# Hand-overs between row halves: new places, SyncE or VectorE, and 17 more of them, in a hand-ordered attention and MoE kernel

## The chip, the cores and the metric

The kernel runs on one core of one Trainium2 chip. The metric is the device time of one execution in microseconds (us); less is better. A core has five engines that run side by side, each with its own in-order queue, and that signal each other by semaphores: TensorE (PE: matmuls, and PEld, the loading of their weights), VectorE (DVE), ScalarE (ACT), GpSimd (POOL) and SyncE (SP). SyncE computes nothing here; it issues DMAs and waits.

## The reference

Softcapped attention over 8 batches, 12 heads, 448 tokens and a head size of 64, and on its result a layer that takes the larger of two products and multiplies it by a third matrix:

```python
scores = scale * (q @ k.T)                 # per batch and head, 448 x 448
scores = cap * tanh(scores / cap)          # cap = 30
attn   = softmax(scores)
x      = attn @ v                          # rearranged to 3584 tokens x 768
out    = maximum(x @ w1, x @ w2) @ w_out   # w1, w2: 768 x 1024, w_out: 1024 x 768
```

Inputs and output are float32; the kernel works in bfloat16 with float32 sums.

## The kernel before

*What is computed.* The maximum is written as x @ w2 + relu(x @ (w1 - w2)), and x @ w2 @ w_out is one product with a matrix wm = w2 @ w_out that is made at the start. The attention goes by pairs of heads i (48 of them), and two pairs make a t (24). For each pair: scores `S` (line 514), tanh `T` (519) and exp `E` (536) on ScalarE, with `L`, `TL`, `EL` for the 64 left-over rows; sums of the exponentials by adds on VectorE (`A` at 548, `B` at 553) and a product with ones (`Y`, "the totals", 573); the product with v (`VL` at 600, `V` at 606); the inverse of the totals (`Y1` to `Y3`, 578 to 584); and the scaling `N` (618, 621) into xT. Scores lie in two PSUM tiles, so that new scores wait until ScalarE has read old ones.

*The second part* has 120 groups of matmuls, numbered through: for each of 8 batches 8 groups of stage 1 (x times a slice of w1 - w2, 6 steps of 448 columns, ended by a relu on VectorE at line 666, `ev`) and 6 or 8 of stage 2 (a slice of the output: 6 steps with wm and 8 with w_out, 384 columns, ended by a copy at 700 or 702, and stored by SyncE at 676 to 681, `st`). Each group sums in one PSUM bank; there are four banks for groups, totals and the like (`O g bank` opens group g).

*Row halves.* A matmul with 64 rows uses half of TensorE's rows, and two such matmuls, one on each half, run at the same time. So each step of a group is cut into its upper and its lower 64 rows, and `M x y n` runs n steps of the upper half of group x and of the lower half of group y, in turn (line 645; 640 is a whole step). A group therefore does one half of all its steps first and the other half later, or goes to and fro: it is transferred from one row half to the other 145 times in all.

*The hand-over.* [...] A hand-over of group g is an empty instruction on another engine (line 654): `Hs g` puts it on SyncE, `H g` on VectorE. It waits for the last matmul of the old half, and the first weight load of the new half waits for it. Since TensorE's queue is in order, a late hand-over stops all that stands behind that weight load. Where no hand-over is written, nothing waits, and only the matmuls in between keep the two apart.

```python
        def step(self, h):
            ...
            ins = nc.tensor.matmul(self.ps, w[r], x[r], start=first, stop=self.at == [self.n, self.n]).ins
            if self.last is not None and self.last[0] != h:
                if self.turn is not None:
                    tc.add_manual_dep(ins, self.turn.name, BANK, reason="bank")
                self.turn = None
            self.last = (h, ins)

        def hand_over(self, eng):

            self.turn = eng.nop().ins
            tc.add_manual_dep(self.turn, self.last[1].name, BANK, reason="bank")
```

*What sets the order.* There is no scheduler: `ORDER`, a string at the top of the file, lists all steps, and each engine's queue takes its instructions in this order. So the place of an `Hs` sets what stands before and behind it on SyncE: other hand-overs, the stores, and from t = 5 on the DMA transposes (`cr`, line 475), which turn q and k from kqs into qkT. A transpose waits for its loads and for its buffer; the loads of a later t (`lk`, `lq`, 328, issued by GpSimd) wait until the transpose has read theirs. The place of an `H` sets what stands around it on VectorE.

Of the kernel before, what the change touches and what calls it, by code (L numbers as in the profile page):

```python
# [21 lines left out]
S 5 0; X 6 0; E 4 0 3; T 5 0; EL 2; Y1 1; Y2 1; PC 2 1; Y3 1; N 1 1; N 1 0; XC 6; X 7 2; W 4 1; S 5 2; S 5 1;
X 8 0; P 3 1 3; WC 4; XC 8; PC 3 1; T 5 1; T 5 2; OP 4 0 1; P 4 0 2; OP 0 1 0; P 0 1 3; S 6 0; S 6 1; W 5 3;
P 0 1 1; P 4 0 6; P 0 1 4; E 5 0 2; T 6 1; T 6 0; E 5 2 3; XC 7; sub 2 0; WC 5; sub 4 0; PC 4 0; sub 0 0; PC 0 1;
OP 5 1 3; P 5 1 4; S 6 2; L 3; Y 2 1; T 6 2; TL 3; E 6 0 3; VL 2; V 2 1 0 1; V 2 0 0 3; V 2 1 1 3; S 7 0; P 5 1 4;
OP 5 0 0; P 5 0 8; Y1 2; Y2 2; Y3 2; N 2 0; N 2 1; A 3 0 1; A 3 0 2; PC 5 1; PC 5 0; T 7 0; EL 3; lk 9 0; lq 11 0;
lv 3 1; lq 9 0; lw1 1; lw1 3; lq 10 0; lk 12 1; lv 3 0; lw1 5; lk 10 0; lk 11 0; lk 11 1; lk 10 1; S 7 2; O 0 1;
M 0 -1 2; S 7 1; M 0 -1 4; O 1 2; M 1 -1 1; T 7 2; T 7 1; Hs 0; M 1 -1 1; S 8 1; M 1 -1 1; M 1 0 3; S 8 0; X 9 3;
OP 4 1 0; P 4 1 4; sub 1 0; sub 3 0; XC 9; T 8 1; E 7 0 2; T 8 0; E 7 2 3; P 4 1 4; L 4; O 2 3; M 2 0 3; S 8 2;
M 2 1 3; A 3 1 1; B 3 1; PC 4 1; ev 0; B 3 0; Hs 2; TL 4; T 8 2; O 3 0; M 3 1 3; M 3 2 1; S 9 0; M 3 2 2; T 9 0;  # L30
E 8 0 3; ev 1; A 3 1 2; sub 5 0; cr 5; Hs 3; O 4 1; M 4 2 1; VL 3; V 3 0 0 3; Y 3 2; V 3 1 0 3; M 4 2 2; S 9 1;
M 4 3 3; lk 13 0; lk 13 1; lv 4 1; lv 4 0; lv 5 3; lv 5 0; lq 13 0; lq 15 0; lq 12 0; lk 12 0; lk 15 1; Y1 3;
Y2 3; Y3 3; ev 2; Hs 4; O 5 2; M 5 3 3; M 5 4 3; T 9 1; EL 4; ev 3; N 3 0; N 3 1; Hs 5; O 6 3; M 6 4 3; M 6 5 2;
# [745 lines left out]
```

## Time and profile before

| what | value |
|---|---|
| time, three executions | 328.19, 328.49, 328.52 us; median 328.49 |
| span of the profiled execution (first to last instruction) | 326.9 us |
| median beyond that span | 1.59 us |
| busy: TensorE, ScalarE, VectorE, GpSimd | 320.2, 281.1, 240.1, 162.2 us |
| matmuls | 4138 |
| hand-overs on SyncE, on VectorE | 107, 21 |

In the profile a row of a timeline has the start and the duration in us, the engine, the line, the operation with what it writes and reads, and a count. A row of the views of waits says who waited for whom: total us, times, the longest. "SPq" and "DVEq" are the engines' queues: instructions that wait or issue and do no work. A busy TensorE is not TensorE at its peak, since matmuls overlap.

### The profile page before, as it was taken

What the parts mean: (1) busy time and instruction counts of PE and PEld (TensorE: products, weight loads), DVE (VectorE), ACT (ScalarE), POOL (GpSimd) and SP (SyncE); (2) the same over time, 40 slices, a digit from 0 to 9 for tenths busy, and PEclk for the clock granted to TensorE, in tenths of its full rate; (3) what the DMA queues carried; (4) which work ended last, traced back from release to release, by engine and by line L of the source; (5) the groups of instructions that cost most, each with busy time, mean ns of one, the idle gap of its engine ahead of it and who ended that gap; (6) DMA issues with size and microseconds to landing.
All of it is one profiled execution on the core that took longest, in us unless ns stands there. A gap on an engine that the chain in (4) does not pass through costs nothing.

```text
span 326.9 us, 9772 instructions
## 1 busy us (share of the span) xinstructions
PE 320.2 (98%) x4138; PEld 184.5 (56%) x4138; DVE 240.1 (73%) x422; ACT 281.1 (86%) x278; POOL 162.2 (50%) x237
## 2 busy tenths in 40 slices
PE   7999999999999999999999999999999999999994
PEld 3454545545656664565565565556466556557662
DVE  3346899987997778987897788968878779773201
ACT  5999999999999999999999999999999999921120
POOL 7357584568772772764774474478448311000000
PEclk9999999999999999999999999999999999999999
DMA  8999999899999999999999999999999963013033
GB/s 179 174 202 185 269 256 112 92 140 116 221 188 98 134 182 191 102 99 175 163 176 108 208 114 181 128 140 182 183 116 101 201 156 45 2 50 98 0 98 96
DMA packets 134508, 46.28 MB, mean 142 GB/s; under 512 B 112321, under 2 KB 129473, under 8 KB 134465
## 3 DMA queue, kind: packets, MB, share of 16 engines
q0 software_dynamic: 94592, 25.02, 78.3%
q1 hardware_dynamic: 39424, 19.99, 31.1%
q8 instruction: 32, 0.52, 0.6%
q10 hardware_dynamic: 448, 0.66, 0.5%
q14 instruction: 12, 0.09, 0.1%
HBM read 47.78 MB, written 11.01 MB: 180 GB/s over the span
## 4 chain that ended last, share of the span: by engine, by line
PE 93%; DMA 3%; POOL 1%; DVE 1%; issue 0%
PE mm L645 61%; PE s L514 9%; PE s L606 9%; PE mm L431 5%; DMA w2b<-in_moe_w_dram 3%; PE s L528 2%; PE s L600 2%; PE mm L573 2%; PE mm L640 1%; POOL kqs L321 1%; PE mm L458 1%; PE mm L566 1%; PE mm L416 0%; DVE xT L621 0%; POOL w2b L366 0%; DVE xT L618 0%
## 5 line engine op out<-in xcount | busy, mean ns | idle before, releaser
L519 ACT ACTIVATE e<-s 128x896 bf16<-128x896 f32 x144 | 125.5, 927 | 5.7 <-PE s L514 5.2
L536 ACT ACTIVATE e<-e 128x1792 bf16<-128x1792 bf16 (+2 forms) x72 | 122.7, 1709 | 0.0
L645 PE MATMUL mm<-wo_sb,gT 64*128 64x384 bf16 x864 | 115.2, 323 | 0.0
L645 PE MATMUL mm<-wm_sb,xT 64*128 64x384 bf16 x648 | 102.2, 323 | 0.0
L645 PE MATMUL mm<-xT,wd_sb 64*128 64x448 bf16 x768 | 97.5, 349 | 0.0
L328 POOL DMA_DIRECT2D kqs<-in_k_dram x76 | 54.7, 722 | 56.1 <-DMA qkT<-kqs 50.9
L645 PEld LDWEIGHTS <-gT 64*128 64x128 bf16 x864 | 58.6, 94 | 25.5 <-issue 1.1
L645 PEld LDWEIGHTS <-wd_sb 64*128 64x128 bf16 x768 | 48.8, 94 | 26.7 <-issue 2.1
L645 PEld LDWEIGHTS <-xT 64*128 64x128 bf16 x648 | 50.3, 94 | 18.5 <-issue 0.2
L514 PE MATMUL s<-qkT 64*128 64x448 bf16 x288 | 52.7, 352 | 0.2 <-DVE xT L618 0.2
L352 POOL DMA_DIRECT2D vp<-in_v_dram x48 | 30.5, 639 | 32.6 <-PE s L514 23.5
L666 DVE TENSOR_SCALAR gT<-mm 128x448 bf16<-128x448 f32 x64 | 38.9, 617 | 8.7 <-PE mm L645 7.6
L328 POOL DMA_DIRECT2D kqs<-in_q_dram x38 | 35.1, 924 | 5.7 <-issue 2.5
L606 PE MATMUL s<-e,vp 128*32 128x448 bf16 x576 | 36.1, 354 | 0.0
L548 DVE TENSOR_TENSOR esum<-e 128x896 bf16<-128x896 bf16 x42 | 25.9, 617 | 9.1 <-ACT e L536 9.1
L621 DVE TENSOR_TENSOR xT<-s,inv 64x448 bf16<-64x448 f32 x48 | 29.9, 622 | 1.7 <-PE s L606 0.8
L548 DVE TENSOR_TENSOR esum<-esum,e 128x896 bf16<-128x896 bf16 x42 | 26.2, 623 | 5.9 <-ACT e L536 4.8
L514 PEld LDWEIGHTS <-qkT 64*128 64x128 bf16 x288 | 18.5, 94 | 20.1 <-issue 12.0
L700 ACT COPY osb<-mm 128x384 f32<-128x384 f32 x10 | 4.8, 479 | 26.9 <-PE mm L645 26.7
L702 DVE COPY osb<-mm 128x384 f32<-128x384 f32 x44 | 23.3, 554 | 6.2 <-PE mm L645 5.7
L553 DVE TENSOR_TENSOR esum<-esum,el 64x896 bf16<-64x896 bf16 x42 | 26.0, 619 | 1.2
L578 DVE STREAM_TRANSPOSE st<-mm 128x448 f32<-128x448 f32 x24 | 15.6, 649 | 13.0 <-PE mm L573 11.3
(57 smaller groups left out, 269.7 us busy)
## 6 DMA issues: line engine op xcount, KB each, us to landing
out_dram<-osb SPq DMA_DIRECT2D x54, 192.0 KB, 4.5
vp<-in_v_dram POOLq DMA_DIRECT2D x38, 160.0 KB, 4.3
kqs<-in_q_dram POOLq DMA_DIRECT2D x46, 112.0 KB, 5.8
kqs<-in_k_dram POOLq DMA_DIRECT2D x76, 56.0 KB, 4.4
osb<-in_moe_w_dram POOLq DMA_DIRECT2D x4, 512.0 KB, 7.4
w2b<-in_moe_w_dram POOLq DMA_DIRECT2D x6, 256.0 KB, 7.1
wo_sb<-in_moe_w_out_dram POOLq DMA_DIRECT2D x4, 384.0 KB, 9.9
vp<-in_v_dram POOLq DMA_DIRECT2D x10, 128.0 KB, 7.7
```

Source lines behind the costliest of these rows:

```text
L328: nc.gpsimd.dma_start(out=to, in_=x)
L352: nc.gpsimd.dma_start(out=to, in_=x)
L514: scored[i, j] = nc.tensor.matmul(s[:, h, :S], k_of(t, o, h, j), q_of(t, o, h)).ins
L519: nc.scalar.activation(expo[i][:, 2 * j : 2 * j + 2, :], slots[i, j][:, :, :S], AF.Tanh, scale=scale / cap)
L536: nc.scalar.activation(e, e, AF.Exp, scale=float(cap))
L548: nc.vector.tensor_add(d, e[:, 0:2, :] if j == 1 else d, e[:, 2 * j : 2 * j + 2, :])
L553: nc.vector.tensor_add(d, d, left_e[t][r, :, :])
L606: nc.tensor.matmul(vals[t][place(m, u), u, :S], w[:, m, :], expo[2 * t + o][:, 2 * j + h, :], start=False, stop=(j == NJ - 1))
L621: nc.vector.tensor_mul(x[64 - r : 128 - r], vals[t][r : r + 64, u, :S], sums[t, 3][64 - r : 128 - r])
L645: ins = nc.tensor.matmul(self.ps, w[r], x[r], start=first, stop=self.at == [self.n, self.n]).ins
L666: nc.vector.tensor_relu(gT[b // 2][:, f, cs], ps)
L702: nc.vector.tensor_copy(o[:, hs], ps)
```

## The change

All steps of `ORDER` but the hand-overs are the same, in the same order; a count in `M` is split where a hand-over now falls inside it. So every matmul, activation, copy and DMA keeps its place among those of its engine.

All 145 transfers now have a hand-over, where 128 had. 96 are on SyncE (107 before), 49 on VectorE (21). Of the 128, 73 stay on SyncE and 9 on VectorE, 34 go from SyncE to VectorE and 12 from VectorE to SyncE; 19 keep both engine and place. The 17 added ones are those of groups 1, 10, 12, 17, 24, 42, 70, 72, 77, 84 and 87 on SyncE and of 27, 40, 47, 54, 57 and 102 on VectorE, each from the upper to the lower half. In ten of them 25 matmuls of groups lie from the last of the old half to the first of the new one, in seven 9.

The core of the diff, at three places, rows cut to the steps that matter:

```diff
-O 36 1; M 36 34 1; lk 27 0; M 36 34 1; A 10 0 1; Hs 35; M 36 34 1; E 21 0 2; M 36 35 1; S 22 1; ev 34; lk 27 1;
-M 36 35 2; O 37 3; M 37 35 1; A 10 0 2; M 37 35 1; Hs 36; lq 27 0; M 37 35 1; M 37 36 2; T 22 0; ev 35; M 37 36 1;
-O 38 2; M 38 36 1; A 10 1 1; M 38 36 1; Hs 37; cr 12;
+O 36 1; M 36 34 1; H 35; lk 27 0; M 36 34 1; A 10 0 1; M 36 34 1; E 21 0 2; M 36 35 1; S 22 1; ev 34; lk 27 1;
+M 36 35 2; H 36; O 37 3; M 37 35 1; A 10 0 2; M 37 35 1;
...
-M 46 44 1; st 2 1; M 46 44 1; Hs 45; T 26 1; cr 14; B 12 0;
-T 26 2; O 47 0; M 47 45 2; H 46; M 47 45 1;
+M 45 43 2; ev 42; lk 31 1; M 45 43 1; M 45 44 2; ev 43; M 45 44 1; H 45; T 26 0;
...
-Hs 66; lq 39 0; M 67 65 1; M 67 66 2; T 34 0; ev 65; M 67 66 1; O 68 0; M 68 66 1; A 16 1 1; M 68 66 1; Hs 67;
+M 66 65 2; O 67 3; M 67 65 1; H 66; A 16 0 2; M 67 65 1; lq 39 0; M 67 65 1; M 67 66 2; T 34 0; ev 65;
+M 67 66 1; O 68 0; M 68 66 1; H 67; A 16 1 1; M 68 66 1; cr 18;
```

In the second place the hand-over of group 46 follows the transpose `cr 14` on SyncE (`Hs 46`). The one edit outside `ORDER` is in `transposes`, and leaves every call as it was:

```diff
-        if c != 1:
+        if bank is not None:
             turned["qk", i] = mm_tile(bank).bitcast(bf16)
```

More of the change, by code (lines that the diff above doesn't have):

```diff
@@ new lines @@
+E 1 2 3; E 1 0 2; TL 1; T 2 0; EL 0; S 3 0; S 2 2; P 3 0 1; W 0 2; P 3 0 1; X 4 3; T 2 2; T 3 0; VL 0; Y 0 1;
+V 0 0 0 3; V 0 1 0 3; S 3 1; lwo 1 0; lwo 1 1; lq 5 0; lk 5 0; lv 1 0; lv 1 1; lk 8 0; lq 8 0; lq 7 0; lw2 4;
+lv 6 2; lq 6 0; lk 7 0; lk 6 0; lw2 5; lw1 2; lw1 4; lw1 0; lv 2 0; lv 2 1; WC 0; PC 3 0; XC 4; Y1 0; Y2 0;
+Y3 0; N 0 0; N 0 1; E 2 0 3; T 3 1; EL 1; E 3 0 2; OP 0 0 1; P 0 0 2; OP 2 1 2; P 2 1 2; P 0 0 1; OP 1 1 3;
+P 1 1 2; P 0 0 1; P 1 1 2; P 0 0 1; P 1 1 4; S 4 0; S 3 2; X 5 0; P 2 1 4; P 0 0 3; P 2 1 1; XC 5; PC 1 1;
@@ new lines @@
+TL 4; T 8 2; O 3 0; M 3 1 3; M 3 2 1; S 9 0; M 3 2 2; T 9 0; E 8 0 3; ev 1; A 3 1 2; sub 5 0; cr 5; O 4 1;
+M 4 2 1; VL 3; V 3 0 0 3; Y 3 2; Hs 3; V 3 1 0 3; M 4 2 2; S 9 1; M 4 3 3; lk 13 0; lk 13 1; lv 4 1; lv 4 0;
+lv 5 3; lv 5 0; lq 13 0; lq 15 0; lq 12 0; lk 12 0; lk 15 1; Y1 3; Y2 3; Y3 3; ev 2; O 5 2; M 5 3 2; Hs 4;
+M 5 3 1; M 5 4 3; T 9 1; EL 4; ev 3; Hs 5; N 3 0; N 3 1; O 6 3; M 6 4 3; M 6 5 2; S 10 0; M 6 5 1; O 7 0;
+M 7 5 3; Hs 6; ev 4; A 4 0 1; ev 5; M 7 6 2; S 9 2; M 7 6 1; Hs 7; cr 6; E 9 0 2; T 10 0; T 9 2; O 8 1; M 8 6 3;
@@ new lines @@
+M 16 15 1; T 14 2; O 17 2; M 17 15 1; H 16; M 17 15 2; B 6 1; M 17 16 2; E 13 2 3; M 17 16 1; ev 15; O 18 3;
+M 18 16 1; L 7; VL 6; A 6 1 2; st 0 2; TL 7; V 6 0 0 2; V 6 1 0 2; Hs 17; Y 6 0; E 14 0 3; V 6 0 2 3; V 6 1 2 3;
+Y1 6; S 15 0; M 18 16 1; lv 8 0; M 18 16 1; Y2 6; M 18 17 1; Y3 6; M 18 17 1; lv 8 1; M 18 17 1; O 19 0;
+M 19 17 1; Hs 18; M 19 17 1; ev 16; lv 8 2; M 19 17 1; M 19 18 1; T 15 0; N 6 0; M 19 18 2; lv 8 3; O 20 1;
+M 20 18 2; EL 7; ev 17; M 20 18 1; lk 20 0; Hs 19; S 15 1; M 20 19 1; N 6 1; M 20 19 1; T 15 1; M 20 19 1;
@@ new lines @@
+L 8; VL 7; A 7 1 2; TL 8; V 7 0 0 2; V 7 1 0 2; Y 7 2; E 16 0 3; V 7 0 2 3; lk 22 0; V 7 1 2 3; Y1 7; S 17 0;
+M 22 23 1; Hs 24; lv 9 0; M 22 23 1; Y2 7; M 22 23 2; Y3 7; M 22 23 1; lv 9 1; M 22 23 2; O 25 2; M 25 23 1;
+N 7 0; M 25 23 1; lv 9 2; M 25 23 1; T 17 0; M 25 24 1; N 7 1; M 25 24 2; lv 9 3; M 25 24 2; EL 8; M 25 24 1;
+S 17 1; lk 22 1; M 25 24 2; ev 22; M 25 24 1; T 17 1; S 17 2; lq 22 0; M 25 24 1; ev 23; M 25 24 1; O 26 3;
+M 26 24 1; T 17 2; M 26 24 1; H 25; A 8 0 1; S 18 0; M 26 24 1; lk 23 0; M 26 25 1; A 8 0 2; M 26 25 1;
@@ new lines @@
+S 21 2; S 22 0; M 35 34 1; ev 33; T 21 2; M 35 34 1; O 36 1; M 36 34 1; H 35; lk 27 0; M 36 34 1; A 10 0 1;
+M 36 34 1; E 21 0 2; M 36 35 1; S 22 1; ev 34; lk 27 1; M 36 35 2; H 36; O 37 3; M 37 35 1; A 10 0 2; M 37 35 1;
+lq 27 0; M 37 35 1; M 37 36 2; T 22 0; ev 35; M 37 36 1; O 38 2; M 38 36 1; A 10 1 1; M 38 36 1; cr 12;
+M 38 36 1; T 22 1; Hs 37; M 38 37 1; S 22 2; B 10 0; M 38 37 2; Hs 38; T 22 2; O 39 0; M 39 37 1; ev 36;
+M 39 37 2; B 10 1; E 21 2 3; M 39 38 3; ev 37; L 11; VL 10; TL 11; V 10 0 0 2; A 10 1 2; V 10 1 0 2; Y 10 1;
@@ new lines @@
+E 22 0 3; V 10 0 2 3; V 10 1 2 3; Y1 10; lk 28 0; S 23 0; M 39 38 2; Y2 10; M 39 38 1; lv 12 0; M 39 38 1;
+Y3 10; M 39 38 3; lv 12 1; M 39 38 1; N 10 0; O 40 3; M 40 38 2; T 23 0; Hs 39; M 40 38 1; Hs 38; lv 12 2;
+N 10 1; M 40 39 3; M 38 39 1; EL 11; lv 12 3; H 40; M 38 39 1; S 23 1; M 38 39 2; lk 28 1; A 11 0 1; M 38 39 1;
+T 23 1; S 23 2; M 38 39 2; A 11 0 2; lq 28 0; M 38 39 1; T 23 2; O 41 1; M 41 39 1; S 24 0; ev 38; M 41 39 2;
+M 41 40 1; lk 29 0; E 23 0 2; M 41 40 1; ev 39; S 24 1; M 41 40 2; lk 29 1; M 41 40 5; lq 29 0; M 41 40 1;
@@ new lines @@
+M 52 50 1; Hs 51; lk 33 0; M 52 50 1; A 13 0 1; M 52 50 1; M 52 51 1; E 27 0 2; M 52 51 1; lk 33 1; ev 50;
+S 28 1; M 52 51 1; H 52; O 53 1; M 53 51 1; A 13 0 2; M 53 51 1; lq 33 0; M 53 51 1; M 53 52 2; ev 51;
+M 53 52 1; T 28 0; M 53 52 2; A 13 1 1; M 53 52 2; cr 15; M 53 52 1; T 28 1; M 53 52 1; B 13 0; S 28 2;
+M 53 52 2; H 53; B 13 1; O 54 2; M 54 52 1; T 28 2; M 54 52 2; M 54 53 1; Hs 52; E 27 2 3; M 54 53 2; M 52 53 1;
+H 54; L 14; VL 13; A 13 1 2; TL 14; V 13 0 0 2; V 13 1 0 2; Y 13 0; E 28 0 3; V 13 0 2 3; lk 34 0; V 13 1 2 3;
@@ new lines @@
+Y1 13; S 29 0; M 52 53 1; lv 15 0; M 52 53 1; Y2 13; M 52 53 2; Y3 13; M 52 53 1; lv 15 1; M 52 53 2; O 55 0;
+M 55 53 1; N 13 0; M 55 53 1; lv 15 2; M 55 53 1; T 29 0; M 55 54 1; N 13 1; M 55 54 2; lv 15 3; M 55 54 2;
+EL 14; M 55 54 1; S 29 1; lk 34 1; M 55 54 2; ev 52; M 55 54 1; T 29 1; S 29 2; lq 34 0; M 55 54 1; ev 53;
+M 55 54 1; H 55; O 56 3; M 56 54 1; T 29 2; M 56 54 1; A 14 0 1; S 30 0; M 56 54 1; Hs 54; lk 35 0; M 56 55 1;
+A 14 0 2; M 56 55 1; E 29 0 2; M 56 55 1; S 30 1; lk 35 1; M 54 55 5; lq 35 0; M 54 55 3; T 30 0; O 57 1;
@@ new lines @@
+EL 15; lv 16 3; M 59 58 1; S 31 1; M 59 58 2; lk 36 1; ev 56; M 59 58 1; T 31 1; S 31 2; M 59 58 1; ev 57;
+M 59 58 1; lq 36 0; M 59 58 1; T 31 2; M 59 58 1; A 15 0 1; S 32 0; M 59 58 2; A 15 0 2; M 59 58 1; lk 37 0;
+E 31 0 2; O 60 3; M 60 58 1; S 32 1; M 60 58 2; H 59; H 58; lk 37 1; M 60 59 3; Hs 60; M 58 59 1; lq 37 0;
+M 58 59 1; T 32 0; M 58 59 1; A 15 1 1; M 58 59 1; cr 17; M 58 59 2; B 15 0; M 58 59 1; T 32 1; M 58 59 1;
+S 32 2; O 61 1; M 61 59 1; ev 58; M 61 59 1; T 32 2; M 61 59 1; B 15 1; M 61 60 3; Hs 61; st 3 5; E 31 2 3;
@@ new lines @@
+ev 59; O 62 2; M 62 60 3; L 16; ev 60; VL 15; TL 16; V 15 0 0 2; A 15 1 2; V 15 1 0 2; E 32 0 3; M 62 61 1;
+Y 15 0; V 15 0 2 3; V 15 1 2 3; lk 38 0; Y1 15; S 33 0; M 62 61 2; Y2 15; lv 17 0; O 63 3; M 63 61 1; st 3 6;
+Hs 62; Y3 15; M 63 61 2; lv 17 1; M 63 62 1; T 33 0; N 15 0; M 63 62 2; lv 17 2; O 64 0; M 64 62 1; ev 61;
+M 64 62 1; EL 16; M 64 62 1; Hs 63; S 33 1; lv 17 3; N 15 1; M 64 63 3; T 33 1; lk 38 1; O 65 1; M 65 63 2;
+Hs 64; M 65 63 1; M 65 64 1; ev 62; lq 38 0; S 33 2; S 34 0; M 65 64 1; ev 63; T 33 2; M 65 64 1; O 66 2;
@@ new lines @@
+cr 19; M 72 70 2; Hs 70; B 17 0; T 36 1; M 72 71 1; S 36 2; M 72 71 2; B 17 1; M 70 71 1; T 36 2; M 70 71 5;
+st 4 0; E 35 2 3; M 70 71 2; O 73 1; M 73 71 1; ev 70; L 18; VL 17; A 17 1 2; TL 18; Hs 72; V 17 0 0 2;
+V 17 1 0 2; Y 17 3; E 36 0 3; V 17 0 2 3; V 17 1 2 3; Y1 17; S 37 0; lk 42 0; M 73 71 2; Y2 17; M 73 72 2;
+Y3 17; lv 19 0; M 73 72 4; N 17 0; lv 19 1; M 73 72 2; T 37 0; M 73 72 1; N 17 1; M 73 72 1; lv 19 2; M 73 72 1;
+Hs 73; O 74 3; M 74 72 2; EL 18; S 37 1; lv 19 3; M 74 72 1; Hs 72; M 74 73 1; ev 71; M 74 73 1; T 37 1;
@@ new lines @@
+M 82 83 1; Y2 19; M 82 83 2; Y3 19; Hs 84; M 82 83 1; lv 21 1; M 82 83 2; O 85 1; M 85 83 1; N 19 0; M 85 83 1;
+lv 21 2; M 85 83 1; T 41 0; M 85 84 1; N 19 1; M 85 84 2; lv 21 3; M 85 84 2; EL 20; M 85 84 1; S 41 1; lk 46 1;
+M 85 84 2; ev 82; M 85 84 1; T 41 1; S 41 2; lq 46 0; M 85 84 1; ev 83; M 85 84 1; O 86 3; M 86 84 1; T 41 2;
+M 86 84 1; H 85; A 20 0 1; S 42 0; M 86 84 1; lk 47 0; Hs 84; M 86 85 1; A 20 0 2; M 86 85 1; E 41 0 2;
+M 86 85 1; S 42 1; lk 47 1; M 84 85 4; Hs 86; M 84 85 1; lq 47 0; M 84 85 3; T 42 0; O 87 2; M 87 85 1;
@@ new lines @@
+S 43 1; M 89 88 2; ev 86; M 89 88 1; T 43 1; S 43 2; M 89 88 1; ev 87; M 89 88 2; T 43 2; M 89 88 1; A 21 0 1;
+S 44 0; M 89 88 2; A 21 0 2; M 89 88 1; E 43 0 2; O 90 3; M 90 88 1; S 44 1; M 90 88 2; Hs 89; H 88; M 90 89 3;
+M 88 89 2; T 44 0; M 88 89 1; A 21 1 1; M 88 89 1; cr 23; M 88 89 2; B 21 0; M 88 89 1; T 44 1; M 88 89 1;
+S 44 2; H 90; O 91 2; M 91 89 1; ev 88; M 91 89 1; T 44 2; M 91 89 1; B 21 1; M 91 90 3; st 5 5; E 43 2 3;
+ev 89; O 92 0; M 92 90 3; L 22; Hs 91; ev 90; VL 21; TL 22; V 21 0 0 2; A 21 1 2; V 21 1 0 2; E 44 0 3;
@@ new lines @@
+M 92 91 1; Y 21 1; V 21 0 2 3; V 21 1 2 3; Y1 21; S 45 0; M 92 91 1; lv 23 0; M 92 91 1; Y2 21; O 93 3;
+M 93 91 1; st 5 6; Y3 21; Hs 92; M 93 91 1; lv 23 1; M 93 91 1; M 93 92 1; T 45 0; N 21 0; M 93 92 1; lv 23 2;
+M 93 92 1; O 94 1; M 94 92 1; ev 91; M 94 92 1; EL 22; lv 23 3; Hs 93; M 94 92 1; S 45 1; N 21 1; M 94 93 3;
+T 45 1; O 95 2; M 95 93 1; Hs 94; M 95 93 2; M 95 94 1; ev 92; S 45 2; S 46 0; M 95 94 1; ev 93; T 45 2;
+M 95 94 1; O 96 0; M 96 94 2; A 22 0 1; M 96 94 1; Hs 95; E 45 0 2; M 96 95 1; S 46 1; ev 94; M 96 95 2; O 97 3;
@@ new lines @@
+Hs 100; M 98 99 2; EL 23; M 98 99 1; S 47 1; M 98 99 2; A 23 0 1; M 98 99 1; T 47 1; S 47 2; M 98 99 2;
+A 23 0 2; O 101 0; M 101 99 1; T 47 2; M 101 99 2; ev 98; M 101 100 3; ev 99; E 47 0 2; M 101 100 8; O 102 1;
+M 102 100 1; Hs 101; M 102 100 1; E 47 2 3; M 102 100 1; A 23 1 1; H 100; M 102 101 3; B 23 0; VL 23;
+V 23 0 0 2; B 23 1; V 23 1 0 2; A 23 1 2; M 100 101 1; st 6 0; M 100 101 4; Y 23 2; V 23 0 2 3; V 23 1 2 3;
+Y1 23; M 100 101 3; H 102; Y2 23; O 103 2; M 103 101 2; Y3 23; eva 100; M 103 101 1; M 103 102 2; eva 101;
@@ L202 @@
+M 117 115 1; M 117 116 2; eva 115; M 117 116 5; st 7 4; M 117 116 4; M -1 116 2; H 117; M -1 116 1; M -1 117 2;
+H 116; M -1 117 1; M 116 117 8; M -1 117 2; eva 116; M -1 117 1; O 118 1; M 118 118 1; eva 117; M 118 118 6;
+st 7 5; M 118 118 7; O 119 2; M 119 119 2; ev 118; M 119 119 12; ev 119; st 7 6;
 """
```

298 lines of the change are left out of this document (112 added, 186 removed).

## The prediction

> **What bounds the kernel now.** I read the page first, then the busy time by window, then the views of waits, and last the timelines around single hand-overs.
>
> ```profile
> span 326.9 us, 9772 instructions
> PE 320.2 (98%) x4138; PEld 184.5 (56%) x4138; DVE 240.1 (73%) x422; ACT 281.1 (86%) x278; POOL 162.2 (50%) x237
> ACT  5999999999999999999999999999999999921120
> ```
>
> TensorE (PE) fills the span. ScalarE (ACT) is full for 34 of the 40 slices, to about 285 us. Then it is nearly idle and TensorE works off what is left alone.
>
> ```profile
> 189.70:260.00 70.30, 70.30 (x924) 41.22 (x920) 58.09 (x103) 68.39 (x67) 42.66 (x60) 1.00 1.35 153
> ```
>
> This stretch of the middle is 70.30 us long; the fourth busy time, 68.39, is ScalarE's. It idles 1.9 us in 70, so two chains bind each other: TensorE needs score banks that ScalarE has emptied, and ScalarE needs scores. A delay of TensorE counts where ScalarE is waiting for it.
>
> ```profile
> ACT e L519 <- PE s L514: 5.2, 9, 0.8
> SPq L654 <- PE mm L645: 218.7, 103, 48.0
> SPq L475 <- PE mm L645: 19.4, 14, 2.3
> ```
>
> ScalarE waits 9 times for TensorE's scores, 5.2 us in all (total, count, longest). SyncE (SPq) spends 218.7 us in hand-overs (L654), as it should: it stands ready before the matmul ends. The last row is their side effect: 14 of 19 DMA transposes (L475) stood behind hand-overs, 1.4 us each on average.
>
> ```profile
> L654 SPq EVENT_SEMAPHORE  x107: 17/17/17, 49.6 to 315.9; - x107
> L654 DVEq EVENT_SEMAPHORE  x21: 21/21/21, 64.5 to 299.6; - x21
> ```
>
> All hand-overs of before: 107 on SyncE, 21 on VectorE (DVE), none before 49.6 us. So nothing changes in the first 49 us.
>
> **The change part by part.** No matmul, activation, copy or DMA changes its place on its own engine; only the waiting instructions move.
>
> *A hand-over on VectorE, by itself.* The one existing case between two adds that run back to back:
>
> ```profile
> 64.18 0.32 PE L645 MATMUL mm<-wm_sb,xT 64*128 64x384 bf16 x1
> 64.11 0.61 DVE L548 TENSOR_TENSOR esum<-e 128x896 bf16<-128x896 bf16 x1
> 64.65 0.62 DVE L548 TENSOR_TENSOR esum<-esum,e 128x896 bf16<-128x896 bf16 x1
> ```
>
> The matmul ends at 64.50, the hand-over fires at once (64.5, the first of VectorE's in the row above) although the add of 64.11 still runs to 64.72, and the next add starts at 64.65, overlapping the first by 0.07. So VectorE's waiting instruction does not wait for the add before it to end, and it costs nothing unless the matmul is late: then the next VectorE instruction starts about 0.1 us after the firing. Against SyncE the hand-over itself comes a few hundredths later (21 against 17 ns for the instruction; I take 0.02).
>
> *Can TensorE bear 0.02?* A weight load runs ahead of its matmul:
>
> ```profile
> 204.39 0.09 PEld L645 LDWEIGHTS <-wd_sb 64*128 64x128 bf16 x1
> 204.57 0.35 PE L645 MATMUL mm<-xT,wd_sb 64*128 64x448 bf16 x1
> ```
>
> It starts 0.18 before the matmul and takes 0.09, so a hand-over, which the weight load waits for, may be 0.09 late unseen. I take 0 for the 40 moves to VectorE (34 from SyncE, 6 new), and keep 0 to 0.02 for the last two, in the tail. The 12 moves back to SyncE gain the same 0.02 at most: 0.
>
> *The 17 added ones.* Ten sit where 25 matmuls lie between the halves, seven where 9 do. Nearest price: an added signal on a matmul.
>
> ```profile
> L645 PE MATMUL mm<-xT,wd_sb x768: 346/349/360, 48.1 to 304.1; 64*128 64x448 bf16 x192
> ```
>
> Minimum, median, maximum: matmuls that signal are among these 768, and none is over 11 ns above the median. So 17 cost between 0 and 17 x 0.011 = 0.19 us; I take 0, the median.
>
> [...]
>
> *What VectorE's queue pays.* I held each of the 49 against the timeline: when its matmul is done against when the next VectorE instruction starts. Most lie in VectorE's idle time, or are followed by some before TensorE asks for a result. Three places are not. The largest is groups 66 and 67, one after the other:
>
> ```profile
> L654 SPq EVENT_SEMAPHORE  x1: 17/17/17, 203.6 to 203.6; - x1
> L654 SPq EVENT_SEMAPHORE  x1: 17/17/17, 204.7 to 204.7; - x1
> 203.46 0.61 DVE L548 TENSOR_TENSOR esum<-esum,e 128x896 bf16<-128x896 bf16 x1
> 204.20 0.62 DVE L666 TENSOR_SCALAR gT<-mm 128x448 bf16<-128x448 f32 x1
> 204.75 0.61 DVE L548 TENSOR_TENSOR esum<-e 128x896 bf16<-128x896 bf16 x1
> ...
> 207.88 0.62 DVE L548 TENSOR_TENSOR esum<-esum,e 128x896 bf16<-128x896 bf16 x1
> 208.31 0.61 PE L573 MATMUL mm<-esum,ones 128*32 128x448 bf16 x4
> ...
> 212.04 0.35 PE L514 MATMUL s<-qkT 64*128 64x448 bf16 x2
> 212.44 0.92 ACT L519 ACTIVATE e<-s 128x896 bf16<-128x896 f32 x1
> ```
>
> On SyncE they fired at 203.6 and 204.7. On VectorE the first stands ahead of the add of 203.46, which then starts at 203.7 (+0.25); the gap of 0.13 up to 204.20 and the overlap of 0.07 eat 0.20 of it. The second stands ahead of the add of 204.75, which then starts at 204.85 (+0.1). From there VectorE has no gap to 207.88, the last sum before the totals: its 0.62 ends at 208.50, and L573's four matmuls, begun at 208.31, take 0.61 because two of them wait for it (0.36 where none does, below). So TensorE is 0.1 late, the scores of 212.04 too, and ScalarE, which starts the tanh of 212.44 only when they are there, passes it on: **+0.11**. Group 36 likewise:
>
> ```profile
> L654 SPq EVENT_SEMAPHORE  x1: 17/17/17, 133.3 to 133.3; - x1
> 133.12 0.61 DVE L548 TENSOR_TENSOR esum<-esum,e 128x896 bf16<-128x896 bf16 x1
> 137.55 0.62 DVE L548 TENSOR_TENSOR esum<-esum,e 128x896 bf16<-128x896 bf16 x1
> ```
>
> The add goes from 133.12 to 133.4; after the same gap and overlap 0.05 is left, and VectorE runs on to the sum of 137.55, which the totals wait for in the same way: **+0.05**. Group 45:
>
> ```profile
> L654 SPq EVENT_SEMAPHORE  x1: 17/17/17, 157.2 to 157.2; - x1
> 157.13 0.62 DVE L548 TENSOR_TENSOR esum<-e 128x896 bf16<-128x896 bf16 x1
> 160.28 0.63 DVE L548 TENSOR_TENSOR esum<-esum,e 128x896 bf16<-128x896 bf16 x1
> 161.11 0.36 PE L573 MATMUL mm<-esum,ones 128*32 128x448 bf16 x4
> ```
>
> The add of 157.13 goes to 157.3, some 0.2 later, and no gap follows up to the sum of 160.28. That ends at 160.91, 0.2 before the totals, less some hundredths for the signal: **+0.03**.
>
> *SyncE.* Nine of the 19 transposes lose hand-overs ahead of them and can be issued 1 to 3 us sooner. In this trace no matmul waits for one: 0. In exchange some hand-overs now stand behind an issue:
>
> ```profile
> 157.53 2.65 SPq L475 DMA_TRANSPOSE qkT<-kqs  x1
> L475 SPq DMA_TRANSPOSE qkT<-kqs x19: 1296/1655/2655, 55.3 to 262.6; - x19
> L654 DVEq EVENT_SEMAPHORE  x1: 21/21/21, 158.6 to 158.6; - x1
> L681 SPq DMA_DIRECT2D out_dram<-osb x46: 466/590/1676, 78.1 to 319.2; - x46
> L654 SPq EVENT_SEMAPHORE  x1: 17/17/17, 127.8 to 127.8; - x1
> L654 SPq EVENT_SEMAPHORE  x1: 17/17/17, 129.0 to 129.0; - x1
> ```
>
> Group 46's hand-over (158.6, on VectorE before) goes to SyncE behind the transpose of 157.53. That can now start some 1.1 earlier, at about 156.4, and with the median 1.66 is through at 158.1: in time, **0**. With 2.65 it ends at 159.1, 0.4 late after the 0.09. And two stores now stand between the hand-overs of groups 32 and 33 (127.8 and 129.0): 2 x 0.59 end at 129.0, just in time; with one of 1.68 they end at 130.1, about 0.7 late after the slack before the next weights. Both ends stay in the range.
>
> *Sum:* 0.11 + 0.05 + 0.03 + 0.02 = 0.21 us on the profiled span of 326.9. The timed median of 328.49 lies 1.59 beyond the span, outside the instructions, and I leave that as it is: **328.7 us**.
>
> **The rivals.**
>
> *1. Slower: SyncE comes late.* One mechanism: a hand-over queued behind an issue that drags or waits for its own load, with TensorE's in-order queue standing meanwhile. It decides at group 46 from a transpose that ends after 158.9, and at group 33 from a long store. Prices 0.4 and 0.7, or up to 1.0 at group 46 if its loads land at 157.2; with the 0.2 that is 329.3 to 329.8. For it: issue times in the same order differ by a factor of two to three. Against: only one of 19 took 2.65.
>
> *2. Faster: transfers are late in the timed runs.* Then transposes issued sooner spare TensorE a wait.
>
> ```profile
> 67.85 1.86 SPq L475 DMA_TRANSPOSE qkT<-kqs  x1
> 73.20 0.37 PE L514 MATMUL s<-qkT 64*128 64x448 bf16 x2
> DMA to landing us min/median/max: 4.2/6.7/10.0
> ```
>
> This transpose is read 5.35 us after its issue, less than the median landing of 6.7. At the median it would be 1.35 late, and the one ahead of it (freed of group 2's hand-over) moves it up, through the loads queued on GpSimd. Then 328.7 - 1.35 = 327.3; with half of it 328.0. Against: it landed in time in this execution, and the three timed ones (328.19 to 328.52) lie within 0.33.
>
> *3. Each added signal costs TensorE.* By the rows at most 0.19: 328.9.
>
> *4. It does nothing,* because ScalarE's idle time or a gap on VectorE takes the 0.2: 328.5.
>
> **How the numbers follow.** A measurement of this kernel can tell about 0.2%, 0.66 us, from no change: 327.83 to 329.15. Forecast 0.30 and rivals 3 and 4 with 0.05 and 0.15 lie within: 0.50. Rival 1 has 0.32, nearly all beyond 329.15. Rival 2 has 0.18 beyond 327.83. The likeliest cases alone span 328.4 to 329.0. The range that leaves out 2 in 10 takes in most of both rivals: 327.5 to 329.8.
>
> **What would show it.** Right: the totals (L573) near 208.3 and 138 start or stretch 0.1 and 0.05 later against the scores before them; SyncE's transposes near 55, 98, 122, 134, 204 are issued 1 to 3 us sooner; waits of TensorE for SyncE stay absent. Rival 1: a gap of TensorE at L645 near 158.8 or 129.3, with an issue on SyncE ending in it. Rival 2: the profile is unchanged or longer while the timed median falls. Wrong altogether: matmul records at hand-overs that stretch everywhere, or ScalarE's idle time growing evenly.

## The result, and the profile after

| | before | changed |
|---|---|---|
| median of 20 executions | 328.58 us (327.80 to 329.81) | 329.35 us (328.46 to 330.04) |
| ratio, 95% interval | 1 | 1.0024 (1.0015 to 1.0032) |
| span of the profiled execution | 326.9 us | 327.7 us |

The changed kernel is slower by 0.24%, 0.79 us (0.49 to 1.05). The forecast of 0.21 us lies below that interval, and the time lies in the range of 327.5 to 329.8.

The page of the changed kernel first, its span and busy times:

```profile
span 327.7 us, 9787 instructions
PE 321.0 (98%) x4136; PEld 184.8 (56%) x4138; DVE 240.7 (73%) x422; ACT 281.0 (86%) x278; POOL 161.7 (49%) x237
```

No engine has more instructions of work than before (two of TensorE's 4138 matmuls left no record), but TensorE counts 0.8 us more as busy and VectorE 0.6. What has changed is seen in the busy times of the stretch from 55 to 285 us, where ScalarE binds (columns as in the prediction; the fourth time is ScalarE's). Before:

```profile
55.00:285.00 230.00, 230.00 (x3004) 133.88 (x3002) 192.80 (x339) 223.88 (x217) 127.75 (x179) 1.00 1.24 141
```

and after:

```profile
55.00:285.00 230.00, 229.69 (x2994) 133.49 (x2992) 192.40 (x338) 223.01 (x215) 127.42 (x179) 1.00 1.22 141
```

TensorE now has 0.31 us in which it does nothing, where it had none, and ScalarE has done 0.87 us less by the same time. Of the 0.31, 0.17 are at group 46 and 0.11 just before 189.55, behind the fourth place below. The views of waits of the changed kernel:

```profile
ACT el L534 <- PE s L530: 1.8, 7, 0.6
PEld L647 <- SPq L656: 0.6, 1, 0.6
```

The last row is new: a weight load waited once for a hand-over (L656; lines are 2 higher than before) on SyncE, 0.6 us. The first is who paid: ScalarE's waits for the scores of the left-over rows, 1.2 us in all before. The hand-overs themselves:

```profile
L656 SPq EVENT_SEMAPHORE  x96: 17/17/17, 49.5 to 312.1; - x96
L656 DVEq EVENT_SEMAPHORE  x49: 21/21/21, 54.7 to 316.6; - x49
```

The wait is at group 46, rival 1's place. Timelines there, SyncE, TensorE and ScalarE of the changed kernel:

```profile
154.22 2.03 SPq L683 DMA_DIRECT2D out_dram<-osb  x2
156.55 2.69 SPq L477 DMA_TRANSPOSE qkT<-kqs  x1
...
157.88 1.29 PE L647 MATMUL mm<-xT,wd_sb 64*128 64x448 bf16 x11
159.35 0.93 PE L647 MATMUL mm<-xT,wd_sb 64*128 64x448 bf16 x7 [0.17 <-SPq L656]
...
159.10 0.99 ACT L538 ACTIVATE e<-e 128x896 bf16<-128x896 bf16 x1
160.66 0.92 ACT L534 ACTIVATE el<-s 128x896 bf16<-128x896 f32 x1 [0.56 <-PE s L530]
```

and TensorE's and ScalarE's of before:

```profile
158.03 1.88 PE L645 MATMUL mm<-xT,wd_sb 64*128 64x448 bf16 x18
...
159.25 1.00 ACT L536 ACTIVATE e<-e 128x896 bf16<-128x896 bf16 x1
160.30 0.92 ACT L532 ACTIVATE el<-s 128x896 bf16<-128x896 f32 x1
```

The transpose cr 14 starts at 156.55, when the two stores ahead of it (2.03 us for both here) are through. This execution is 0.15 us ahead of before's, so in before's time that is 156.70, 0.3 later than reckoned (156.4). It takes 2.69 us and ends at 159.24. The hand-over behind it fires then, and the 18 matmuls that were one row of before break in two. ScalarE, 0.15 us ahead of before at 159.1, is 0.36 behind at 160.7: **0.51 us**.

The two places that the forecast named, the totals (L575) near 138 and 208 and the tanh that waits for them, changed:

```profile
137.77 0.68 PE L575 MATMUL mm<-esum,ones 128*32 128x448 bf16 x4
208.94 0.75 PE L575 MATMUL mm<-esum,ones 128*32 128x448 bf16 x4
...
213.19 0.92 ACT L521 ACTIVATE e<-s 128x896 bf16<-128x896 f32 x1 [0.18 <-PE s L516]
```

and before (the other one, 208.31, is in the prediction):

```profile
137.98 0.61 PE L573 MATMUL mm<-esum,ones 128*32 128x448 bf16 x4
```

They stretch by 0.07 and 0.14 us (0.61 to 0.68, 0.61 to 0.75), and ScalarE loses 0.07 and 0.13. A fourth place is not in the prediction. VectorE and then ScalarE, changed:

```profile
186.50 0.65 DVE L586 STREAM_TRANSPOSE inv<-rs 128x448 f32<-128x448 f32 x1
187.60 0.62 DVE L620 TENSOR_TENSOR xT<-s,inv 128x448 bf16<-128x448 f32 x1 [0.46 <-DVE inv L586]
...
196.12 0.92 ACT L534 ACTIVATE el<-s 128x896 bf16<-128x896 f32 x1 [0.29 <-PE s L530]
```

and before:

```profile
186.14 0.65 DVE L584 STREAM_TRANSPOSE inv<-rs 128x448 f32<-128x448 f32 x1
186.89 0.62 DVE L618 TENSOR_TENSOR xT<-s,inv 128x448 bf16<-128x448 f32 x1
...
195.49 0.92 ACT L532 ACTIVATE el<-s 128x896 bf16<-128x896 f32 x1 [0.19 <-PE s L528]
```

The scaling L620 starts 0.46 us after the inverse is done, where it took 0.10, with no hand-over between the two; ScalarE is 0.63 behind before at 196.1, and was 0.36 behind up to there: **0.26 us** (unrounded).

So the profile's account of ScalarE against before: 0.18 ahead up to 55 us (the two executions begin differently, before the change's first effect), then +0.07, +0.51, +0.26, +0.13, and 0.76 behind at its end (some hundredths go elsewhere).

### The profile page after: what moved, and what is told of

The parts are those of the page before. It is cut to its first block, busy times and chain, and to the rows that moved or that the text cites. A ratio compares the mean times of both kernels' runs of the same rounds, so it can differ in the third digit from the quotient of the medians.

```text
span 327.7 us, 9787 instructions
## 1 busy us (share of the span) xinstructions
PE 321.0 (98%) x4136; PEld 184.8 (56%) x4138; DVE 240.7 (73%) x422; ACT 281.0 (86%) x278; POOL 161.7 (49%) x237
## 4 chain that ended last, share of the span: by engine, by line
PE 94%; ACT 2%; DVE 2%; issue 1%; SPq 0%; DVEq 0%
PE mm L647 60%; PE s L516 9%; PE s L608 9%; PE mm L433 5%; PE s L530 2%; PE mm L575 2%; PE s L602 2%; PE mm L642 1%; PE mm L473 1%; PE mm L460 1%; ACT e L521 1%; DVE xT L623 1%; ACT e L538 1%; PE mm L568 1%; PE mm L418 0%
## 6 DMA issues: line engine op xcount, KB each, us to landing
w2b<-in_moe_w_dram POOLq DMA_DIRECT2D x6, 256.0 KB, 6.7
```

## The experiments

The theory (A): hand-overs cost by place, and SyncE's at group 46 is the largest, as rival 1 had it. Against it (B): the loss is made of many small ones, signals and queue instructions. Line numbers of the first four kernels are lower, since their ORDER is wrapped to fewer lines: by 11 in those from the changed kernel, by 8 and 7 in b_46sp and b_17. Since executions differ by up to 0.7 us in how they begin, places are read against the same execution's own state just ahead of them.

**a_46dve**: the changed kernel, group 46 back on VectorE.

```diff
-M 46 45 1; Hs 46; T 26 2; O 47 0; M 47 45 3;
+M 46 45 1; T 26 2; O 47 0; M 47 45 2; H 46; M 47 45 1;
```

> The changed kernel, but group 46's hand-over stands on VectorE again, at its place of before. Theory A, SyncE comes late (rival 1): the 0.17 us gap of TensorE ahead of its matmuls at 159.35 goes, ScalarE idles 0.05 instead of 0.56 us ahead of the tanh of the left-over rows (160.66), and the time falls by 0.5 us: ratio to before 1.0009 instead of 1.0024. Theory B, the loss is made of many small ones (added signals, VectorE's queue) and this one gap would be eaten by later idle time: the time stays, 1.0024, and the idle time turns up elsewhere within some 10 us.

```profile
155.79 3.43 SPq L466 DMA_TRANSPOSE qkT<-kqs  x1
...
158.05 1.88 PE L636 MATMUL mm<-xT,wd_sb 64*128 64x448 bf16 x18
...
160.32 0.92 ACT L523 ACTIVATE el<-s 128x896 bf16<-128x896 f32 x1
```

SyncE, TensorE, ScalarE: the transpose takes even longer, 3.43 us, and ends at 159.22 as in the changed kernel, but the 18 matmuls are one row and ScalarE's row shows no idle time ahead of the tanh: no hand-over stands behind the issue. Ratio 1.0005 (0.9994 to 1.0016). A holds, B doesn't. The 0.26 us near 187 are gone as well, which nothing explained yet.

**b_46sp**: the kernel before, with only this hand-over put behind the transpose.

```diff
-M 46 45 1; T 26 2; O 47 0; M 47 45 2; H 46; M 47 45 1;
+M 46 45 1; Hs 46; T 26 2; O 47 0; M 47 45 3;
```

> The kernel before, with one edit: group 46's hand-over goes to SyncE behind the transpose cr 14, as in the changed kernel. Here group 45's hand-over still stands ahead of that transpose, so it is issued at 157.5. Theory A: with this transpose's own 2.65 us it is through at 160.2, 0.96 later than the 159.24 of the changed kernel, so ScalarE loses 0.51 + 0.96 = 1.5 us: ratio 1.0045. If its duration is free to fall to the median of 1.66, it is through at 159.2 and costs 0.5: 1.0015. Theory B (the place does not decide): within 0.1 us of before, 1.000.

```profile
157.44 2.30 SPq L467 DMA_TRANSPOSE qkT<-kqs  x1
...
159.85 0.93 PE L637 MATMUL mm<-xT,wd_sb 64*128 64x448 bf16 x7 [0.61 <-SPq L646]
...
159.16 1.00 ACT L528 ACTIVATE e<-e 128x896 bf16<-128x896 bf16 x1
161.16 0.92 ACT L524 ACTIVATE el<-s 128x896 bf16<-128x896 f32 x1 [1.00 <-PE s L520]
```

One hand-over moved, and the kernel before is about as slow as the changed one: 1.0035 (1.0022 to 1.0049). The transpose took 2.30, between the two durations that I had put in; ScalarE lost 0.95 by its starts (0.09 ahead to 0.86 behind), between 0.5 and 1.5.

**a_366667sp**: the changed kernel, with `Hs 36`, `Hs 66` and `Hs 67` at their places of before instead of `H 36`, `H 66` and `H 67`.

> The changed kernel, with the hand-overs of groups 36, 66 and 67 on SyncE again, at their places of before. If VectorE's queue pays for them as forecast: ScalarE's idle time ahead of the tanh at 142 and 212 shrinks by 0.07 and 0.13 us, sum -0.2: ratio to before 1.0018 instead of 1.0024. If the idle time of later places would have taken it back: 1.0024. If VectorE's queue pays far more than the profile of one run shows: under 1.0012.

```profile
133.58 1.84 SPq L466 DMA_TRANSPOSE qkT<-kqs  x1
135.53 0.36 PE L636 MATMUL mm<-xT,wd_sb 64*128 64x448 bf16 x1 [0.47 <-SPq L645]
...
156.82 3.61 SPq L466 DMA_TRANSPOSE qkT<-kqs  x1
...
161.85 0.92 ACT L523 ACTIVATE el<-s 128x896 bf16<-128x896 f32 x1 [1.10 <-PE s L519]
```

A miss: 1.0040 (1.0026 to 1.0054), no gain. The tanhs near 142 and 212 wait no longer, as expected, but with group 36 on SyncE again the transpose cr 12 is issued at 133.58 instead of 131.20, and group 37's hand-over, which the change had put *behind* it, is late: ScalarE loses 0.68. The same happens behind cr 18 (0.66). (The profiled execution took 330.63 us, where the median of the eight is 329.71, so these losses are larger than the usual ones.) A move to VectorE and a place behind a transpose belong together; I had undone one half.

**b_17**: the kernel before and the 17 added hand-overs alone, of which one is shown.

```diff
-TL 13; V 12 0 0 2; V 12 1 0 2; Y 12 1; E 26 0 3;
+TL 13; V 12 0 0 2; V 12 1 0 2; Y 12 1; H 47; E 26 0 3;
```

> The kernel before with the 17 added hand-overs alone, each on the engine and at the place that it has in the changed kernel. Forecast: nothing, ratio 1.0000, ScalarE's start times within 0.1 us of before all along. [...]

```profile
L638 PE MATMUL mm<-xT,wd_sb x768: 346/349/360, 47.5 to 303.5; 64*128 64x448 bf16 x192
L638 PE MATMUL mm<-wm_sb,xT x648: 319/322/333, 62.5 to 315.9; 64*128 64x384 bf16 x162
```

Minimum, median and maximum of the first group are those of before, to the nanosecond, and its first and last start lie 256.0 us apart, as before (48.1 and 304.1); all 17 added hand-overs fire between them. ScalarE is 0.63 us ahead of before's already at 25 us, before the first of them, and still 0.63 at its end. Ratio 1.0002 (0.9988 to 1.0015). The interval alone would allow rival 3's 0.19 us (1.0006); the profile doesn't, since all of it would have to show between those two starts.

**after_r**: the changed kernel again, for a second profile.

> The changed kernel once more, unchanged, for a second profile and a time beside the next three. Theory A: TensorE's gap behind the transpose cr 14 is there again, and ScalarE's loss ahead of the tanh near 160.3 is again the end of that issue less 158.88 us (the due time by which three profiles agree: 159.24, 160.43 and 159.74, less what each was already late, lost 0.51, 1.05 and 0.96). Ratio to before 1.0015 to 1.0032. The gap of 0.46 us of VectorE ahead of L620 at 187.60, with no waiting event beside it, either recurs (then it belongs to the change: its 0.26 us on ScalarE counts) or not (then it belongs to that one execution).

```profile
155.19 3.25 SPq L477 DMA_TRANSPOSE qkT<-kqs  x1
...
158.68 1.00 ACT L538 ACTIVATE e<-e 128x896 bf16<-128x896 bf16 x1
159.87 0.92 ACT L534 ACTIVATE el<-s 128x896 bf16<-128x896 f32 x1 [0.19 <-PE s L530]
...
186.80 0.62 DVE L620 TENSOR_TENSOR xT<-s,inv 128x448 bf16<-128x448 f32 x1 [0.46 <-DVE inv L586]
```

Ratio 1.0028 (1.0014 to 1.0043), though the span of this execution is 326.9 as before's: it began 0.63 us sooner. Group 46 cost 0.14 here, and VectorE's gap is the same 0.46 at the same instruction, so it belongs to the kernel. The four late executions give the due time of that hand-over:

| run | issue ends | shift: ScalarE at its previous start, against before (159.25) | ScalarE idles | end less shift less idle |
|---|---|---|---|---|
| changed | 159.24 | -0.15 | 0.56 | 158.83 |
| after_r | 158.44 | -0.57 | 0.19 | 158.82 |
| b_46sp | 159.74 | -0.09 | 1.00 | 158.83 |
| a_366667sp | 160.43 | +0.50 | 1.10 | 158.83 |

From that point on, each hundredth of a microsecond of the issue is one of ScalarE. With ScalarE's usual 0.05 of idle time there, the loss starts at 158.88.

**a_mend**: the changed kernel with groups 35, 36, 37, 45, 46, 65, 66 and 67 as before.

> The changed kernel with the hand-overs of groups 35, 36, 37, 45, 46, 65, 66 and 67 at their engines and places of before, so that the whole neighbourhood of the transposes cr 12, cr 14 and cr 18 is as before; the other 137 stay as changed. If the three places found make the whole loss: 0.06 + 0.51 + 0.13 = 0.70 us less than the changed kernel, ratio to before 1.0000 within 0.1%, no wait of TensorE for SyncE. If the loss is spread over the 137 others: 1.001 to 1.0024.

```profile
134.25 1.81 SPq L477 DMA_TRANSPOSE qkT<-kqs  x1
...
137.22 0.92 ACT L534 ACTIVATE el<-s 128x896 bf16<-128x896 f32 x1 [0.47 <-PE s L530]
```

Ratio 1.0008 (0.9995 to 1.0022), undecided, and the profile says why: group 38, `H 38` before and `Hs 38` behind cr 12 in the changed kernel, was not among the eight and is now late, 0.48 us.

**a_swap** and **a_store**: the changed kernel, with the transpose, or the two stores ahead of it, moved behind group 46's hand-over.

```diff
-T 26 1; cr 14; B 12 0; M 46 45 1; S 26 2; M 46 45 1; ev 44; M 46 45 1; Hs 46;
+T 26 1; B 12 0; M 46 45 1; S 26 2; M 46 45 1; ev 44; M 46 45 1; Hs 46; cr 14;
```

```diff
-M 46 44 1; st 2 1; M 46 44 1; T 26 1; cr 14; B 12 0; M 46 45 1; S 26 2; M 46 45 1; ev 44; M 46 45 1; Hs 46;
+M 46 44 2; T 26 1; cr 14; B 12 0; M 46 45 1; S 26 2; M 46 45 1; ev 44; M 46 45 1; Hs 46; st 2 1;
```

> The changed kernel, with the transpose cr 14 moved behind group 46's hand-over on SyncE; the hand-over keeps engine and place. Theory A (the place in SyncE's queue decides, not the engine): the 0.17 us gap of TensorE goes and the time falls by 0.5 us as with the hand-over on VectorE: ratio 1.0008. The transpose is issued at 158.8, 2.2 later; its result is needed only some 10 us later: no cost. Theory B (SyncE is slower than VectorE to fire): the gap stays, 1.0024.

> The changed kernel, with the two stores ahead of the transpose cr 14 moved behind group 46's hand-over. What the transpose waits for is there by 154.1, so it can be issued then instead of 156.55, and even with 3.6 us it is through at 157.7: no gap, -0.5 us, ratio 1.0008. If the long issues of this transpose (2.69, 3.43 and 3.61 us where it directly follows the two stores, 2.26, 2.30 and 2.65 where 1.5 to 1.9 us lie between) come from the stores ahead of it, it falls to 1.3 to 2.2 us; if they come from what runs beside it at this place, it stays at 2.3 or more.

```profile
158.80 1.81 SPq L477 DMA_TRANSPOSE qkT<-kqs  x1
...
160.18 0.92 ACT L534 ACTIVATE el<-s 128x896 bf16<-128x896 f32 x1
```

That is a_swap; SyncE of a_store:

```profile
154.35 1.56 SPq L477 DMA_TRANSPOSE qkT<-kqs  x1
```

Both lose nothing at group 46, with the hand-over on SyncE as it was: 1.0009 (1.0001 to 1.0018) and 1.0012 (1.0003 to 1.0021). So it is the place in the queue, not the engine. What is left of the loss is the 0.07, 0.26 and 0.13 of the other places, and 0.05 near 166.5, the price of group 45 on VectorE (0.03 forecast), which in the changed kernel hides behind group 46.

**a_mend2**: as a_mend, with groups 38 and 68 as before too.

> As a_mend, and groups 38 and 68 at their engines and places of before too, since in a_mend the hand-over of group 38 still stood behind the transpose cr 12 (through at 136.06) and ScalarE lost 0.48 us at 136.9. If the places found make the whole loss: TensorE waits for SyncE nowhere, ScalarE's start times follow those of before within 0.15 us from 50 us to the end, ratio 1.0000 (0.9993 to 1.0007). If the 135 others cost something that no single place shows: 1.0007 to 1.0015.

```profile
L647 PE MATMUL mm<-wm_sb,xT x648: 319/322/333, 63.0 to 316.3; 64*128 64x384 bf16 x162
```

Ratio 1.0000 (0.9991 to 1.0009); first to last start 253.3 us as before (changed: 254.2), and ScalarE is 0.17 us ahead of before's both at 25 us and at its end. 133 of the 145 hand-overs are the changed kernel's (groups 38 and 68 have two each), and cost nothing. Nor do they gain: the transposes cr 9 and cr 11, for example, are issued at 96.23 and 118.80 in it, 2 and 3 us sooner than before (98.26, 121.98).

The gap near 187 was left. It was there in four profiles (changed, after_r, a_swap, a_store) and absent in the others. Counting VectorE's rows in the trace, its queue's waiting instructions included, the delayed scaling is the 320th in those four, and the 307th, 308th, 313th (312th in the expectation below), 318th, 319th or 321st in others. Theory P: the place in VectorE's instruction stream. Theory T: what runs beside it in the changed kernel.

**a_swap_1dve**: as a_swap, and group 1's hand-over on VectorE (`Hs 1` becomes `H 1`).

> As a_swap, with group 1's hand-over on VectorE instead of SyncE: one more instruction in VectorE's queue, at 50 us, where VectorE has time. Theory P, the gap of 0.46 us ahead of the scaling L620 near 187 hangs on the place in VectorE's instruction stream (the scaling is the 320th VectorE row of the trace in the four profiles that show the gap, the 308th, 312th, 318th, 319th or 321st in those that don't): here it is the 321st, the gap falls to 0.10 and ScalarE's 0.26 us between 189 and 196 go. Theory T, it hangs on what runs beside it at that time in the changed kernel: it stays, with its 0.26.

```profile
L656 DVEq EVENT_SEMAPHORE  x1: 21/21/21, 50.6 to 50.6; - x1
...
50.71 1.23 DVE L404 TENSOR_TENSOR wd_sb<-osb,w2b 128x1024 bf16<-128x1024 f32 x1 [0.97 <-DMA kqs<-in_k_dram]
```

The gap near 187 is 0.10 again and ScalarE loses nothing there: P. But the time is 1.0043 (1.0030 to 1.0056), my mistake: at 50 us VectorE has no time. The hand-over fires at 50.60, and the subtraction L404, queued behind it, starts at 50.71, 0.97 after the cast ahead of it ends (49.74); in a_swap it follows that cast without a gap, at 49.88. ScalarE loses 1.1 us by it from 54 to 56. (The DMA that the row names isn't the cause; the waiting instruction is.)

**b_12dve** and **b_13dve**: the kernel before, with 12 of the moves to VectorE, chosen so that the scaling becomes the 320th; and with group 36 as a thirteenth, which is shown.

```diff
-O 37 3; M 37 35 1; A 10 0 2; M 37 35 1; Hs 36; lq 27 0;
+H 36; O 37 3; M 37 35 1; A 10 0 2; M 37 35 1; lq 27 0;
```

> The kernel before, with 12 of its SyncE hand-overs (groups 2, 14, 21, 22, 25, 28 second, 29, 35, 44, 45, 52, 55) on VectorE at their places of the changed kernel. My reckoning of VectorE's queue gives 0 for eleven and 0.03 for group 45. Theory P: the scaling L618 near 186.6 becomes the 320th VectorE row, so the gap of 0.46 us appears in this kernel too and ScalarE loses 0.26 us between 189 and 196. Theory T: no such gap; all within 0.05 us of before.

> As b_12dve, with group 36 on VectorE as well: one instruction more. Forecast: ScalarE loses 0.06 at 141.9 (VectorE's queue). Theory P: the scaling is the 321st row, the gap near 187 is 0.10 and ScalarE loses nothing there, so this kernel with one more push is 0.2 us quicker at its end than b_12dve, against its own start. Theory T: both behave alike near 187.

b_12dve:

```profile
186.66 0.62 DVE L618 TENSOR_TENSOR xT<-s,inv 128x448 bf16<-128x448 f32 x1 [0.47 <-DVE inv L584]
```

b_13dve:

```profile
186.44 0.62 DVE L618 TENSOR_TENSOR xT<-s,inv 128x448 bf16<-128x448 f32 x1
257.13 0.62 DVE L618 TENSOR_TENSOR xT<-s,inv 128x448 bf16<-128x448 f32 x1 [0.46 <-DVE inv L584]
```

P, twice over: put on place 320, the scaling of the kernel before has the gap too, and ScalarE loses 0.3 us from 189 to 196. One instruction more and it is gone there, and another scaling, now the 448th row, 128 further on, has it at 257 with the same loss after it (0.28). So my expectation for b_13dve, quicker at its end, was wrong, though the theory was right. Ratios 1.0008 (0.9999 to 1.0016) and 1.0010 (0.9997 to 1.0023).

## Why the prediction was wrong in its size

- *Two chains bind each other; nothing before 49 us.* Right. Every loss found is one of TensorE or VectorE where ScalarE had at most 0.2 us to spare. (Two profiles, a_46dve and a_mend, lose 0.14 to 0.15 us more near 90; the changed kernel's two don't, and its cause is open.)
- *A hand-over on VectorE costs nothing unless the matmul is late, then 0.1 us after the firing.* Right: a_swap_1dve, 50.60 to 50.71.
- *The 17 added ones: 0.* Right (b_17). Rival 3 is out.
- *VectorE's queue pays at three places, 0.11, 0.05 and 0.03.* Right, a little small: 0.13, 0.07 and 0.05, the last hidden in the changed kernel.
- *Group 46, "with the median 1.66 is through at 158.1: in time, 0".* **This step failed.** The point of decision (158.88 against 158.9) was right; the duration was not this transpose's. Its own row showed 2.65, and wherever it stood right behind the two stores, as the change puts it, it took 2.69 to 3.61 (six profiles). A median over 19 transposes at 19 places says little about one of them. The start was one number too, 156.4, where the stores ahead of it moved it: in before's time it was 156.70 in the changed kernel (2.03 us for both stores) and 155.76 in after_r (1.10 us). Cost: 0.51 and 0.14 us in these two profiles. That rival 1's price of 0.4 lies between is partly luck: it counts from 158.6 + 0.09, and from the rival's own 158.9 the same 2.65 us would cost 0.2.
- *The remaining moves to VectorE: 0.* Right for their waits, **and yet incomplete**: more instructions shift everything behind them in VectorE's stream, and 12 of the 28 pushed one scaling from place 308 to 320. Cost 0.26 us; neither the sum nor a rival had it.
- *Group 33 behind two stores: 0.* Right; no profile shows it late.
- *Transposes issued 1 to 3 us sooner: 0 here* (and rival 2, up to 1.35 us in the timed runs). They are sooner, cr 11 at 118.77 instead of 121.98 in the changed kernel, and nothing is gained: a_mend2 keeps cr 9 and cr 11 sooner, and the one at 67.85 that rival 2 named too (66.23), and is at 1.0000 (0.9991 to 1.0009), so rival 2's gain of 0.2 to 0.4% didn't come.
- *Span and median.* The changed median lies 1.65 beyond its span, 1.59 assumed.

Sum from the two profiles without their beginnings: 0.07 + 0.51 + 0.26 + 0.13 = 0.97 and 0.05 + 0.14 + 0.27 + 0.13 = 0.59; their mean is 0.78, the measured loss 0.79. That two profiles 0.38 apart match it so closely is luck. Rival 1 came true at group 46, not at group 33: 0.33 us on average of the two. The rest of what the sum lacked, 0.26, is the place in the stream, which no rival had.

## What to carry to other kernels

A waiting instruction moved behind a DMA issue inherits that issue's duration: take it from the row of that very issue, as a range, compare its end with the point from which the waiter counts, and leave room, since the new place can change the duration (here 2.65 before, 2.69 to 3.61 after) and the issues ahead of it move its start. Undo or move such edits in pairs; a place behind an issue was safe here only as long as what stood ahead of the issue stayed away (a_366667sp lost 0.68 and 0.66 us by one half undone, a_mend 0.48). And where a change adds instructions to a queue, look at what they push onto places where a run has shown a delay (here the 320th and the 448th of VectorE's, 0.35 us), since the row of such a loss names only the engine's own earlier result.

## What the runs showed of the hardware

*On the 320th and the 448th place of VectorE's stream a scaling starts 0.35 us late.* The gap behind the inverse is 0.46 to 0.47 us there instead of 0.10, in six profiles of six in which a scaling stands there. On the 384th place (a_mend2) and on the 512th (changed, after_r, a_swap, a_store) a scaling has the usual 0.10. The 512th, changed:

```profile
291.14 0.65 DVE L586 STREAM_TRANSPOSE inv<-rs 128x448 f32<-128x448 f32 x1
291.89 0.62 DVE L620 TENSOR_TENSOR xT<-s,inv 128x448 bf16<-128x448 f32 x1
```

Just ahead of such a scaling the queue has waited for the engine's own result: 18 of the 24 of L620 in the changed kernel have a waiting row, 21 ns each, and the one of the delayed scaling stands at 187.2, 0.4 us ahead of its start (187.60). Whether other instructions on such places have the same delay, covered by the one that still runs, no run here shows. The view of the DMA queues from 186 to 189 us in the changed kernel (packets, MB, share) has a row

```profile
q14 instruction: 1, 0.01, 1.2%
```

one packet, and none of q8; the page has for the whole run

```profile
q8 instruction: 32, 0.52, 0.6%
q14 instruction: 11, 0.09, 0.1%
```

The view from 186 to 188.2 us has no row of either: the packet on q14 starts only after that, when the delayed scaling (187.60, 0.62 us long) is nearly over, so it is not what the scaling waited for. The two late places lie 128 apart; what makes them late, no run here shows.

*The transpose cr 14 takes longer directly behind two stores.* Issued 0.3 to 0.5 us after them it took 2.69, 3.25, 3.43, 3.61, 2.96 and 2.93 us; 1.4 to 2.1 us after them 2.15 to 2.65; without them (a_store) 1.56, and behind the hand-over, 3.46 us after them, 1.81 (a_swap). So when it was issued sooner, without group 45's hand-over at its front, it was also longer, in all six. Loads and the other DMAs beside it differ in these runs too; which of them does it stays open.
